# A Trainium2 kernel of two spectral and two dense layers: first layernorm from the token rows, and finer waits at three seams

## The chip, the cores and the metric

The kernel runs on one core of one Trainium2 chip. The metric is the device time of one execution in microseconds (us), taken as the median of three runs. One execution was also recorded by the profiler, and all durations below come from that record unless a sentence says otherwise. Engine names are those of the profile: PE (matrix engine), PEld (its weight loads), DVE (vector engine), ACT (scalar engine), POOL and SP. A name with a q (SPq, POOLq, ACTq) stands for instructions in that engine's queue that issue DMAs.

## What is computed

```python
x = A_x                                       # 2048 x 1024, bf16
x = x + A(layernorm(x))                       # spectral layer
x = x + B(layernorm(x))                       # dense layer
x = x + A(layernorm(x))
x = x + B(layernorm(x))
# A(x): irfft2(rfft2(x) * (w_r + 1j*w_i)), over tokens and features
# B(x): (h * tanh(softplus(h))) @ w2  with  h = x @ w1 + b1, w1 1024 x 3584
# layernorm: (x - mean) / sqrt(var + 1e-5) over the 1024 features, no gain
```

## The kernel before

Tokens stay in SBUF as `XS`, 16 tiles of 128 tokens by 1024 features. The spectral layer does not start from `XS`. It starts from `XR`, in which a partition holds a pair (a residue of the token index, a block h of 128 features), so that each token's row lies on eight partitions. In the first layer `XR` is loaded straight from `A_x` in four quarters of 32 token columns, 8 DMAs each (`prologue`, L372). In the second it is filled from `XN` rows: the dense layer before it normalises each tile of tokens (`apply`, L493), POOL stores the tile to a DRAM scratch (`xn_store`, L505), and POOL loads it back turned (`xr_load`, L514). Tile 15 alone goes from SBUF to SBUF (`xr_direct`, L518): 8 DMAs dealt to SP, ACT and POOL in turn. `xn_out` is a ring of two buffers.

**First normalisation.** The first step s1 is 16 groups j of 8 matmuls each, 128 columns wide. The mean needs no work there, and the scale 1/sqrt(var+eps) is put into the weights: `scaled` (L586) makes 8 scaled copies of the 128 x 128 table `M0` in one DVE instruction. The variances come out of `XR` itself: per quarter q, `squares` (L552) squares the quarter on ACT (the first on DVE), `sums` (L557) adds over features by two rows of 16 matmuls against a block-ones table `BO`, `roots` (L574) reduces and takes the root. `s1_first` (L606) writes this order out by hand: quarter q+1 is prepared while the four groups of quarter q run, and `s1_evac` (L602) copies each group's PSUM to `Y`, on ACT but for two. `XS` is loaded later, 1 MB in front of the layer and 1 MB behind each of its first three steps (L880 to L883), only for the residual.

**The spectral pipeline.** After s1, eight groups g pass through s2, s3, i1 and i2, software-pipelined over 11 steps (L862 on). In the first layer `filter_bins` (L902) also builds the filter of each group from rows of `w_r` and `w_i`, which POOL loads into a ring of two (`load_wr`, L894). Every engine gets its instructions in program order, and a group waits by semaphore for exactly the resources (`Res`) that its operands name.

**Turn to the tokens.** i2 leaves group g in `U`; `u_turn` (L832) stores it to a DRAM scratch and `u_back` (L847) reads it turned into rows g, g+8, ... of `UT`. For the last group the store is cut in two halves of its 16 rows (L839), both from ACT, and the read back in two halves of the 128 columns dl, on SP and ACT (L848). The whole of `UT` is one `Res`, so the first inverse matmul `i4` (L935, PE line L943) waits for all of it. The DVE adds of L957 and the next layernorm follow.

**The dense layer** is PE at work almost without a break: L1018 (first matmul, Mish on ACT) and L1036 (second matmul, DVE adds at L1041). The last four tiles of the first dense layer close with `mm2(3, t, h)`, `apply`, and the stores and loads above (L1177 to L1186).

Of the kernel before, what the change touches and what calls it, by code (L numbers as in the profile page):

```python
# [7 lines left out]
P = 128  # L8
# [116 lines left out]
def make_tables():  # L125
# [40 lines left out]
    def by_group(t):  # L166
# [5 lines left out]
                ident=np.eye(P), BO=np.kron(np.eye(16), np.ones((8, 8))))  # L172
# [7 lines left out]
class KB:  # L180
# [122 lines left out]
    def build(self):  # L303
# [3 lines left out]
        self.con = {k: v.ap().bitcast(BF) for k, v in con.items()}  # L307
        self.u_d = nc.dram_tensor("u_scratch", (8, P, 16, P), BF, kind="Internal").ap()
# [3 lines left out]
        with ExitStack() as es:  # L312
# [27 lines left out]
            self.r_ud = [Res(f"ud{i}") for i in range(8)]  # L340
            self.r_wd = [Res(f"wd{i}") for i in range(8)]
# [17 lines left out]
    def layout(self):  # L359
        K = 1024  # L360
        self.o = dict(XR=0, Z=0, X=12 * K, T=20 * K, YK=28 * K, V=40 * K, JT=48 * K, M0=49 * K, BO=49 * K + 256, RT=50 * K, XQ=32 * K,
                      ST=51 * K, WR=54 * K, YS=56 * K, UT=64 * K, MN=64 * K, Y=96 * K, XN=128 * K, U=128 * K,
                      FT=140 * K, BT=144 * K + 512, WT=self.W1_OFF)
        self.ob = dict(AT0=0, AT1=36 * K, XT1=28 * K, XT0=120 * K, W2=64 * K, JUNK=54 * K)
        assert 149 * K <= self.W1_OFF, (149 * K, self.W1_OFF)
# [6 lines left out]
    def prologue(self):  # L372
        sp = self.sp
        self.op(self.pool, lambda e: e.memset(self.EPS[:], 1e-5), writes=[self.r_eps, self.r_warm])
        small = {}

        def load_small(name, n, prog=sp):
            b = self.alloc(name, self.o[name], [n])
            self.dma(prog, b.ap, self.con[name], name.lower(), writes=[b.res])
            small[name] = b  # L380

        self.XR = self.alloc("XR", self.o["XR"], [P, P])
        self.r_xr = []
        xv = self.x[0].rearrange("(n2 n1) (h l) -> h n2 n1 l", n2=16, l=P)
        for q in range(4):
            r = Res(f"xr{q}")
            for h in range(8):
                prog = (sp, self.pool, self.act)[h % 3] if q == 0 else (sp, self.pool)[h % 2]
                self.dma(prog, self.XR.ap[h:P:8, 32 * q:32 * q + 32, :], xv[h][:, 32 * q:32 * q + 32, :], f"xr{q}{prog.name}", parts=[r])
            self.r_xr.append(r)  # L390
            if q == 0:
                load_small("BO", P, self.act)
                load_small("M0", P, self.act)
                self.warm(ACT.Sqrt)
        self.M0, self.BO = small["M0"], small["BO"]
        self.dma(sp, self.FD[:], self.con["FD"], "fd", writes=[self.r_fd])
        load_small("JT", 4 * P)
        self.JT, self.r_jt = small["JT"].ap, small["JT"].res
        self.w1_next = 0

    def load_x(self, c, after):

        xt = self.x[0].rearrange("(t p) d -> p t d", p=P)
        self.dma(self.sp, self.XS[:, 4 * c:4 * c + 4, :], xt[:, 4 * c:4 * c + 4, :], f"x{c}", reads=after,
                 writes=self.r_xs[4 * c:4 * c + 4])
# [99 lines left out]
    def xn_store(self, j, b):  # L505
        b.unread = False
        self.dma(self.pool, self.xn_d[j], b.ap, "xw" + b.res.name[2:], reads=[b.res], writes=[self.r_xnd[j]])

    def open_xr(self):
        self.XR = self.alloc("XR", self.o["XR"], [P, P])  # L510
        self.XR.res.begin()
        self.r_xr = [self.XR.res] * 4

    def xr_load(self, j):  # L514
        self.dma(self.pool, self.XR.ap[row_of(j, 0):row_of(j, 7) + 1:4, :, :], self.xn_d[j].rearrange("n (h l) -> h n l", l=P), f"xl{j % 4}",
                 reads=[self.r_xnd[j]], parts=[self.XR.res])

    def xr_direct(self, j, b):  # L518

        b.unread = False  # L520
        for h in range(8):
            prog = (self.sp, self.act, self.pool)[h % 3]
            self.dma(prog, self.XR.ap[row_of(j, h):row_of(j, h) + 1, :, :], b.ap[:, h * P:(h + 1) * P], "xd" + prog.name,
                     reads=[b.res], parts=[self.XR.res])
# [6 lines left out]
    def copy(self, prog, dst, src, reads, writes, scale=None, parts=()):  # L531
# [6 lines left out]
        return self.op(prog, fn, reads=reads, writes=writes, parts=parts)  # L538

    def open_scales(self):  # L540


        self.XQ = [self.alloc(f"XQ{i}", self.o["XQ"] + i * 8192, [32, P]) for i in range(2)]
        self.ST = self.alloc("ST", self.o["ST"], [4, 4, 32], F32)
        self.RT = self.alloc("RT", self.o["RT"], [P], F32)
        self.MN = self.alloc("MN", self.o["MN"], [P, P])
        self.r_st, self.r_rt, self.r_mn = ([Res(f"{n}{i}") for i in range(k)] for n, k in (("st", 4), ("rt", 4), ("mn", 16)))
        for b, rs in ((self.ST, self.r_st), (self.RT, self.r_rt), (self.MN, self.r_mn)):
            for r in rs:
                r.inherit(b.res)  # L550

    def squares(self, q, prog):  # L552
        x, b = self.XR.ap[:, 32 * q:32 * q + 32, :], self.XQ[q % 2]
        fn = (lambda e: e.activation(b.ap, x, ACT.Square)) if prog is self.act else (lambda e: e.tensor_tensor(b.ap, x, x, ALU.mult))  # L554
        self.op(prog, fn, reads=[self.r_xr[q]], writes=[b.res])

    def sums(self, q, sq):  # L557

        bank = 6 + q % 2
        ps = self.PS[:, bank, 256 * sq:256 * sq + 256].rearrange("p (n l) -> p n l", l=8)  # L560
        src = self.XQ[q % 2].ap if sq else self.XR.ap[:, 32 * q:32 * q + 32, :]
        fns = [lambda e, i=i: e.matmul(ps, self.BO.ap, src[:, :, 8 * i:8 * i + 8], start=(i == 0), stop=(i == 15)) for i in range(16)]  # L562
        rb = self.r_bank[bank]
        if not sq:
            rb.begin()
        w = list(rb.prev.items()) + self.BO.res.wait_r() + (self.XQ[q % 2].res if sq else self.r_xr[q]).wait_r()
        t = None
        for i, fn in enumerate(fns):
            t = self.pe.add(fn, waits=w if i == 0 else (), inc=(i == 15))
        self.mark(self.pe, t, reads=[self.BO.res] + ([self.XQ[q % 2].res] if sq else []), parts=[rb])  # L570

    def roots(self, q):

        dve = self.dve  # L574
        st, rst, rb = self.ST.ap[:, q], self.r_st[q], self.r_bank[6 + q % 2]
        s1, s2, a, b = (st[:, i, :] for i in range(4))
        rc = self.RT.ap[:, 32 * q:32 * q + 32]
        src = self.PS[:, 6 + q % 2, :].rearrange("p (c n l) -> p c n l", c=2, l=8)
        self.op(dve, lambda e: e.tensor_reduce(st[:, 0:2, :], src, axis=mybir.AxisListType.X, op=ALU.add), reads=[rb], writes=[rst])
        self.op(dve, lambda e: e.tensor_tensor(a, s1, s1, ALU.mult), writes=[rst])  # L580
        self.op(dve, lambda e: e.scalar_tensor_tensor(b, a, -1.0 / self.D, s2, ALU.mult, ALU.add), writes=[rst])
        self.op(self.act, lambda e: e.activation(a, b, ACT.Sqrt, bias=self.EPS[:, 0:1], scale=1.0 / self.D), reads=[self.r_eps],
                writes=[rst])
        self.op(dve, lambda e: e.reciprocal(rc, a), reads=[rst], writes=[self.r_rt[q]])

    def scaled(self, j):  # L586
        n = slice(8 * j, 8 * j + 8)
        self.op(self.dve, lambda e: e.tensor_tensor(self.MN.ap[:, n, :], self.M0.ap.unsqueeze(1).to_broadcast([P, 8, P]),
                                                    self.RT.ap[:, n].unsqueeze(2).to_broadcast([P, 8, P]), ALU.mult),
                reads=[self.r_rt[j // 4], self.M0.res], writes=[self.r_mn[j]])  # L590

    def s1_mm(self, li, j, i):
        M, XR = self.M, self.XR
        ps, banks = self.PS[:, 2 * i:2 * i + 2, :].rearrange("p a b -> p (a b)"), [self.r_bank[2 * i], self.r_bank[2 * i + 1]]
        fns = []
        for q in range(8):
            n = 8 * j + q
            m = M[:] if li else self.MN.ap[:, n, :]
            fns.append(lambda e, q=q, n=n, ps=ps, m=m: e.matmul(ps[:, q * P:(q + 1) * P], XR.ap[:, n, :], m, start=True, stop=True))  # L599
        self.group(fns, reads=[self.r_xr[j // 4], self.r_m if li else self.r_mn[j]], writes=banks)  # L600

    def s1_evac(self, j, i, prog):  # L602
        ps, banks = self.PS[:, 2 * i:2 * i + 2, :].rearrange("p a b -> p (a b)"), [self.r_bank[2 * i], self.r_bank[2 * i + 1]]
        self.copy(prog, self.Y.ap[:, :, 8 * j:8 * j + 8], ps.rearrange("p (q k) -> p k q", q=8), banks, [], parts=[self.Y.res])

    def s1_first(self):  # L606
        self.open_scales()
        self.Y = self.alloc("Y", self.o["Y"], [P, P])
        self.Y.res.begin()
        act, dve = self.act, self.dve  # L610
        self.sums(0, 0)
        self.squares(0, dve)
        self.sums(0, 1)
        self.roots(0)
        for j in range(16):
            q = j // 4 + 1
            if q < 4 and j % 4 == 0:
                self.squares(q, act)
                self.sums(q, 0)
# [605 lines left out]
```

## Time and profile before

| | us |
|---|---|
| median of three runs | 1064.42 |
| lowest, highest run | 1061.64, 1064.61 |
| profiled execution: its time | 1064.61 |
| profiled execution: its span | 1062.5 |
| PE, PEld busy | 966.3, 522.9 |
| DVE, ACT, POOL busy | 341.3, 326.0, 72.8 |
| mean granted PE clock | 0.968 |

The span runs from the first to the last instruction; the 2.1 us between it and the execution's time lie outside of it. Times inside the span are counted from its start. In a list of instructions in order of time, a row has its start, its length, its engine, its line and operation, out<-in, the count of merged instructions, and in brackets how long the engine was idle before it and what released it. In the chain of waits a row has start, length and what the chain spent it on.

### The profile page before, as it was taken

The numbers are of one execution on the slowest core, as the hardware profiler recorded it, in microseconds if no ns is written. First come the engines' busy times: TensorE is split into PE (matmuls) and PEld (weight loads), VectorE is DVE, ScalarE is ACT, GpSimd is POOL, SyncE is SP. The second block draws the span as 40 slices with busy tenths as digits, with TensorE's granted clock in tenths as the row PEclk, the third lists the DMA queues.
The fourth block names the chain that finished last, engine by engine and source line by source line (L and its number), as shares of the span: only waits on it lengthen the run. The fifth ranks groups of instructions, "written<-read, shape, count | busy, mean of one in ns | idle before, by whom it ended". The sixth has DMA issues, their size and how long they took to land.

```text
span 1062.5 us, 14272 instructions
## 1 busy us (share of the span) xinstructions
PE 966.3 (91%) x6071; PEld 522.9 (49%) x6160; DVE 341.3 (32%) x678; ACT 326.0 (31%) x443; POOL 72.8 (7%) x117
## 2 busy tenths in 40 slices
PE   4679678999999999999977985899999999999998
PEld 3557566444444444444436765744444444444443
DVE  3568655260443200024325775526011100000111
ACT  3678545333000233410006863533300014341000
POOL 5033000000000000000620200000000000000000
PEclk9889969999999999999998996999999999999999
DMA  9369851446111122000951786045611122200000
GB/s 218 102 228 325 229 141 34 156 157 213 45 46 46 41 80 60 1 11 20 199 101 23 205 210 179 2 151 185 199 44 35 54 67 74 65 1 11 20 20 30
DMA packets 151279, 106.99 MB, mean 101 GB/s; under 512 B 72881, under 2 KB 130353, under 8 KB 151217
## 3 DMA queue, kind: packets, MB, share of 16 engines
q1 hardware_dynamic: 137008, 75.24, 24.7%
q0 software_dynamic: 9776, 28.84, 9.7%
q10 hardware_dynamic: 4432, 2.00, 0.8%
q8 instruction: 49, 0.80, 0.3%
q14 instruction: 14, 0.11, 0.0%
HBM read 80.81 MB, written 20.71 MB: 96 GB/s over the span
## 4 chain that ended last, share of the span: by engine, by line
PE 76%; DVE 7%; DMA 6%; ACT 5%; issue 3%; POOL 2%; SPq 0%; ACTq 0%; DVEq 0%; POOLq 0%
PE PS L1018 36%; PE PS L1036 32%; POOL ARENA L249 2%; PE PS L707 2%; DMA xn_scratch<-ARENA 1%; DVE XS L957 1%; DMA ARENA<-in_A_x_dram 1%; ACT ARENA L554 1%; DMA u_scratch<-ARENA 1%; ACT ARENA L533 1%; DVE ARENA L828 1%; ACT ARENA L759 1%; PE PS L781 1%; DMA ARENA<-u_scratch 1%; DVE ARENA L993 1%
## 5 line engine op out<-in xcount | busy, mean ns | idle before, releaser
L1018 PE MATMUL PS<-ARENA 128*128 128x512 bf16 (+1 forms) x1946 | 391.0, 360 | 10.4 <-DVE ARENA L993 7.2
L1036 PE MATMUL PS<-ARENA 128*128 128x512 bf16 x1756 | 385.5, 379 | 1.9
L1022 ACT ACTIVATE ARENA<-PS,B 128x512 bf16<-128x512 f32 (+1 forms) x248 | 159.7, 645 | 439.3 <-PE PS L1018 439.3
L1018 PEld LDWEIGHTS PS<-ARENA 128*128 128x128 bf16 x1984 | 194.1, 99 | 202.0 <-DVE ARENA L993 8.8
L1036 PEld LDWEIGHTS PS<-ARENA 128*128 128x128 bf16 x1792 | 175.3, 98 | 211.5
L1041 DVE TENSOR_TENSOR XS<-PS,XS 128x512 bf16<-128x512 f32 x64 | 44.3, 692 | 536.9 <-PE PS L1036 536.9
L957 DVE TENSOR_TENSOR XS<-PS,XS 128x512 bf16<-128x512 f32 (+1 forms) x40 | 29.1, 790 | 82.5 <-PE PS L943 82.5
L461 DVE BATCH_NORM_STATS2 BN<-XS 128x6 f32<-128x512 bf16 x84 | 54.7, 677 | 1.2
L943 PE MATMUL PS<-MT,ARENA 128*128 128x32 bf16 (+1 forms) x768 | 24.6, 189 | 27.5 <-DMA ARENA<-u_scratch 24.3
L943 PEld LDWEIGHTS PS<-MT,ARENA 128*128 128x128 bf16 x768 | 23.3, 101 | 31.0 <-issue 25.4
L759 ACT ACTIVATE ARENA<-PS 128x1024 bf16<-128x1024 f32 x32 | 33.3, 1042 | 8.6 <-PE PS L755 8.6
L707 PE MATMUL PS<-FD,ARENA 128*128 128x256 bf16 (+1 forms) x256 | 33.5, 278 | 2.5 <-DVE ARENA L537 1.3
L249 POOL DMA_DIRECT2D xn_scratch<-ARENA x15 | 8.2, 550 | 391.1 <-DVE ARENA L500 391.1
L788 ACT ACTIVATE ARENA<-PS 128x1024 bf16<-128x1024 f32 x32 | 33.3, 1041 | 4.1 <-PE PS L781 4.1
L781 PE MATMUL PS<-ARENA 128*128 128x256 bf16 x256 | 33.2, 273 | 0.5 <-DMA ARENA<-c_bt 0.4
L562 PE MATMUL PS<-ARENA 128*128 128x256 bf16 x128 | 19.4, 319 | 14.7 <-DMA ARENA<-in_A_x_dram 12.0
L433 ACT ACTIVATE RS<-MV,EPS 128x1 f32<-128x1 f32 x6 | 1.7, 289 | 97.1 <-DVE MV L464 96.2
L533 ACT ACTIVATE ARENA<-PS 128x1024 bf16<-128x1024 f32 x23 | 22.4, 1027 | 25.4 <-PE PS L599 25.3
L763 DVE TENSOR_TENSOR ARENA<-ARENA 128x1024 bf16<-128x1024 bf16 x32 | 22.0, 688 | 24.2 <-ACT ARENA L759 24.1
L781 PEld LDWEIGHTS PS<-ARENA 128*128 128x128 bf16 x256 | 24.6, 98 | 10.3 <-DVE ARENA L770 1.0
L707 PEld LDWEIGHTS PS<-FD,ARENA 128*128 128x128 bf16 x256 | 24.5, 100 | 7.9 <-DVE ARENA L537 3.0
L802 PE MATMUL PS<-ARENA,BD 128*128 128x256 bf16 x192 | 25.9, 273 | 1.3 <-DVE ARENA L828 1.1
(74 smaller groups left out, 528.3 us busy)
## 6 DMA issues: line engine op xcount, KB each, us to landing
ARENA<-in_B_w_dram SPq DMA_DIRECT2D x56, 512.0 KB, 4.0
ARENA<-in_B_w_dram SPq DMA_DIRECT2D x56, 256.0 KB, 4.4
u_scratch<-ARENA SPq DMA_DIRECT2D x14, 512.0 KB, 3.5
ARENA<-u_scratch SPq DMA_DIRECT2D x14, 512.0 KB, 6.0
XS<-in_A_x_dram SPq DMA_DIRECT2D x4, 1024.0 KB, 9.7
w_scratch<-ARENA POOLq DMA_DIRECT2D x8, 512.0 KB, 7.1
ARENA<-w_scratch POOLq DMA_DIRECT2D x8, 512.0 KB, 5.7
out_dram<-XS SPq DMA_DIRECT2D x16, 256.0 KB, 2.0
```

Of the source, the lines that this page charges most:

```text
L461: self.op(self.dve, lambda e: e.bn_stats(self.BN[:, j, 6 * h:6 * h + 6], self.XS[:, j, 512 * h:512 * h + 512]), reads=[self.r_xs[j]], part ...
L533: fn = (lambda e: e.activation(dst, src, ACT.Copy)) if scale is None else \
L707: fns.append(lambda e: e.matmul(dst, at(r), FD[:, t:t + n], start=start, stop=stop))
L759: self.op(act, lambda e: e.activation(x.ap.rearrange("p a b -> p (a b)"), ps, ACT.Copy, scale=SIG), reads=banks, writes=[x.res])
L781: fns.append(lambda e, c=c, part=part: e.matmul(ps[:, c * 256:(c + 1) * 256], yk.ap[:, part, c * P:(c + 1) * P], t[:, (128, 0)[part]:(384, ...
L788: self.op(act, lambda e: e.activation(v.ap[:, :, i, :], src, ACT.Copy), reads=banks, parts=[v.res])
L943: fns.append(lambda e, l=l: e.matmul(ps[:, w * l:w * l + w], self.UT.ap[:, u0 + l, :], self.MT[:, 8 * lo:8 * lo + w], start=True, stop=True))
L957: self.op(self.dve, lambda e: e.tensor_tensor(xs, src, xs, ALU.add), reads=rb, parts=self.r_xs[lo:lo + nb])
L1018: fns.append(lambda e, db=db, bank=bank, fl=fl: e.matmul(PS[:, bank, 0:w], wb.ap[:, db, fl * P:(fl + 1) * P], x.ap[:, db, tok], start=(db ...
L1022: self.op(act, lambda e, bank=bank, ft=ft: e.activation(at.ap[:, ft, tok], PS[:, bank, 0:w], ACT.Mish, bias=self.B1[:, ft:ft + 1]), reads= ...
L1036: fns.append(lambda e, i=i, ft=ft: e.matmul(PS[:, bank, :], at.ap[:, ft, t * P:(t + 1) * P], W2[ft].ap[:, h * 512:(h + 1) * 512], start=(i ...
L1041: self.op(dve, lambda e: e.tensor_tensor(xs, PS[:, bank, :], xs, ALU.add), reads=[self.r_bank[bank]], writes=[self.r_xs[j]])
```

## The change

The diff does four things.

1. **First layernorm.** The variances are taken from `XS` instead of `XR`. `XS` is loaded first, by 4 DMAs of 1 MB on SP ahead of everything else; the `XR` quarters follow (quarter 0 all on SP, the others half on SP and half on POOL, POOL's behind the arrival of the last `XS` tile). `first_scales` takes 10 tiles' statistics on DVE and 6 on ACT, then one root for all 16 tiles, one transpose on PE and two copies, which gives `RT`. `scaled` becomes 8 small instructions per group, 5 on DVE and 3 on ACT, issued four groups ahead. The evacuations of s1 alternate between DVE and ACT. The squares, the sums, the roots per quarter, the table `BO`, and the later loads of `XS` with their gates are gone.
2. **Last group's turn.** `UT` has four `Res`, one per quarter of dl. The half 0 of the last group's rows is read back as soon as its store has landed, in two DMAs on SP; half 1 in four DMAs, a quarter of dl each, on ACT and SP in turn. `i4` waits for the quarters that it reads.
3. **Last tile's rows.** `xr_direct` sends 16 DMAs of 64 tokens in place of 8 of 128, first half of the tokens first, and the `XR` of the second layer has one `Res` per half.
4. **Late stores.** `xn_store` of tiles 12 to 14 is issued by SP instead of POOL.

```diff
 def prologue(self):
+    self.warm(ACT.Sqrt)
+    for c in range(4):
+        self.dma(sp, self.XS[:, 4*c:4*c+4, :], xt[:, 4*c:4*c+4, :], f"x{c}", writes=self.r_xs[4*c:4*c+4])
+    load_small("M0", P, BF)
+    load_small("IDF", P, F32)
...
-    prog = (sp, self.pool, self.act)[h % 3] if q == 0 else (sp, self.pool)[h % 2]
+    prog = self.pool if q and h % 2 else sp      # POOL's read self.r_xs[15] first
...
 def xn_store(self, j, b):
-    self.dma(self.pool, self.xn_d[j], b.ap, ...)
+    prog = self.sp if j >= 12 else self.pool
+    self.dma(prog, self.xn_d[j], b.ap, ...)
 def xr_direct(self, j, b):
-    for h in range(8):
-        prog = (self.sp, self.act, self.pool)[h % 3]
-        self.dma(prog, self.XR.ap[row_of(j,h):row_of(j,h)+1, :, :], b.ap[:, h*P:(h+1)*P], ..., parts=[self.XR.res])
+    for i in range(16):
+        half, h = i // 8, i % 8
+        n = slice(64*half, 64*half+64)
+        prog = (self.sp, self.act, self.pool)[i % 3]
+        self.dma(prog, self.XR.ap[row_of(j,h):row_of(j,h)+1, n, :], b.ap[n, h*P:(h+1)*P], ..., parts=[self.r_xr[2*half]])
...
+def first_scales(self):
+    for j in range(0, 16, 4):
+        n = 2 if j % 8 else 3
+        for i in range(n):
+            self.stats_dve(j + i)
+        for i in range(n, 4):
+            self.stats_act(j + i)
+        self.sums_to_mv(j + n, 4 - n)
+    self.root(0, 16)
+    rt = self.alloc("RT", self.o["RT"], [16, 8], F32)
+    self.op(dve, tensor_copy(rt, RS[:, 2, :] broadcast to 16 x 8))
+    self.group([transpose(self.PS[:, 7, 0:P], rt, self.IDF)])
+    self.op(dve, tensor_copy(rt, self.PS[:, 7, 0:P]))
...
 def scaled(self, j):
-    self.op(self.dve, tensor_tensor(MN[:, 8 columns, :], M0 broadcast, RT broadcast, mult))
+    for q in range(8):
+        n = 8 * j + q
+        if q % 3 == 1:
+            self.op(self.act, activation(MN[:, n, :], M0, Copy, scale=rc[:, n:n+1]))
+        else:
+            self.op(self.dve, tensor_scalar(MN[:, n, :], M0, rc[:, n:n+1], None, mult))
 def s1(self, li):
+    for j in range(4 if not li else 0):
+        self.scaled(j)
+    for j in range(16):
+        (8 matmuls of group j; copy to Y on ACT if j is odd, else on DVE)
+        if not li and j + 4 < 16:
+            self.scaled(j + 4)
...
 def u_turn(g, half):                              # g == 7
+    if half == 0:
+        u_back(6)
+    self.dma(act, self.u_d[g][:, h, :], u.ap[:, h, :], ..., writes=[self.r_ud7[half]])
+    if half:
+        u_last()
+def u_last():
+    back(sp, 0, 0, 2)                             # (engine, half of rows, first quarter of dl, quarters)
+    back(sp, 0, 2, 2)
+    for q in range(4):
+        back((act, sp)[q % 2], 1, q, 1)
...
-    if li == 0 and step < 3:
-        gate = Res("gate")
-        gate.set_w(self.pe, self.pe.count)
-        self.load_x(step + 1, [gate])
...
 def i4(...):
-    self.group(fns, reads=[self.UT.res, self.r_mt], writes=rb)
+    self.group(fns, reads=self.r_ut[u0 // 32:(u0 + n - 1) // 32 + 1] + [self.r_mt], writes=rb)
```

## The prediction

> **What bounds the kernel now.** I read the page's 40 slices (26.6 us each) first, to see where PE is not full.
>
> ```profile
> PE   4679678999999999999977985899999999999998
> DMA  9369851446111122000951786045611122200000
> ```
>
> PE is busy 9 tenths or more through both dense layers. The holes are slices 0 to 2 (start), 4 to 6 and 24 (turn to the tokens), 20 and 21 (return to the spectral layer). So a change outside of PE can only win there; I took each hole in order of time. First the list of instructions of 0 to 75 us:
>
> ```profile
> 28.46 3.61 ACT L554 ACTIVATE ARENA<-ARENA 128x4096 bf16<-128x4096 bf16 x1
> ...
> 32.13 1.92 PE L562 MATMUL PS<-ARENA 128*128 128x256 bf16 x16 [0.77 <-ACT ARENA L554]
> ...
> 36.07 4.56 DVE L588 TENSOR_TENSOR ARENA<-ARENA 128x1024 bf16<-128x1024 bf16 x4
> ...
> 57.34 1.89 PE L707 MATMUL PS<-FD,ARENA 128*128 128x256 bf16 x8 [1.32 <-DVE ARENA L537]
> ```
>
> Squares (3.61), their sums (1.92), then roots and four scalings (4.56) form a chain that comes round every 10.8 us, once per quarter: the squares start at 17.6, 28.5 and 39.3. `XR` itself was complete near 22 us, where POOL's wait for quarter 3 ends. The first s2 matmul comes at 57.34 because of this chain, not because of the load. Then the chain of waits:
>
> ```profile
> 61.37 7.51 DMA ARENA<-in_A_w_i_dram
> ...
> 126.58 5.18 DMA u_scratch<-ARENA
> 131.84 4.66 DMA ARENA<-u_scratch
> 136.74 1.03 PE PS L943 x32
> ```
>
> Filter rows for group 2 hold the pipeline up once. At the turn, the last half store and then the whole read back lie bare; the second layer repeats both (5.46 and 4.72). Last, the instructions around 553 us:
>
> ```profile
> 542.17 0.55 DVE L500 TENSOR_SCALAR ARENA<-XS,MV,RS 128x1024 bf16<-128x1024 bf16 x1 [1.07 <-DMA xn_scratch<-ARENA]
> 543.44 0.58 POOL L249 DMA_DIRECT2D xn_scratch<-ARENA  x1
> 548.71 1.09 POOL L249 DMA_DIRECT2D ARENA<-xn_scratch  x1 [4.69 <-DMA xn_scratch<-ARENA]
> 549.79 0.58 POOL L249 DMA_DIRECT2D xn_scratch<-ARENA  x1
> 553.80 1.85 SPq L249 DMA_DIRECT2D ARENA<-ARENA  x3
> 553.80 2.14 ACTq L249 DMA_DIRECT2D ARENA<-ARENA  x3
> 554.77 1.10 POOL L249 DMA_DIRECT2D ARENA<-xn_scratch  x1 [4.40 <-DMA xn_scratch<-ARENA]
> 555.86 1.13 POOL L249 DMA_DIRECT2D ARENA<-ARENA  x2
> 562.52 8.03 PE L599 MATMUL PS<-M,ARENA 128*128 128x128 bf16 x104 [11.62 <-DMA ARENA<-ARENA]
> ```
>
> POOL's queue alternates a store with a load that waits for it. Tile 15 is ready at 553.8, yet tile 14's load and POOL's two direct pieces go out behind it, and s1 starts at 562.52.
>
> **Part 1, the first layernorm.** Prices:
>
> ```profile
> L461 DVE BATCH_NORM_STATS2 BN<-XS 128x6 f32<-128x512 bf16 x84 | 54.7, 677 | 1.2
> L500 DVE TENSOR_SCALAR ARENA<-XS,MV,RS 128x1024 bf16<-128x1024 bf16 x48 | 25.0, 543 | 2.1 <-DMA xn_scratch<-ARENA 1.1
> ```
>
> *Arrival.* A single `XS` megabyte took 8.3 us at best, beside other loads; while three of them ran (62 to 75 us) the DMAs moved about 400 GB/s. At 350 GB/s 1.05 MB is 3.0 us; with 0.74 until SP's first issue, 0.37 for it and some 1.5 until bytes flow (in this profile near 2 us), tiles 0 to 3 are there at 5.6, the last at 14.6. The upper bound is 0.74 + 8.3 = 9.0.
> *Statistics.* In a row at 142 us one tile on DVE takes 1.45 (two half tiles and the aggregate); 10 make 14.5. The three small operations of `sums_to_mv` took 0.53, four times 2.1. From 5.6 that ends at 22.2. ACT's 6 tiles at 2.35 make 14.1 beside it. Then root (0.3), reciprocal (0.25, from 0.35 for 32 columns), copy (0.3), transpose, copy (0.3), four handovers of 0.1: 2.0 to about 24.2. The profile has no f32 transpose: between 0 and 1.9 (the 16 bf16 ones at 146 us); I take 0.4.
> *Scaling and s1.* The 128x128 scaling is not in the profile. On DVE its pace c lies between 0.13 (a statistic behind an aggregate, 143.76 to 143.89) and 0.46 (two L500 rows end to end take 1.00, of 543 ns each). A 128x8 TENSOR_SCALAR takes 172 ns; by size between that and L500 it is 0.22 long, less the 0.08 by which neighbours overlap: 0.14 to 0.19. I take 0.18, nearer to the small row. DVE then has 20c for the first four groups, 12 times 5c for the others, six copies at 1.18 between them and two at the end (2.4): 24.2 + 9.5 + 80c = 48.1. ACT has per two groups six scalings of 0.31 (0.2 fixed, 128 columns of 0.83 ns) and a copy of 0.93, 2.8, under DVE's 3.0. PE's 16 matmuls take 2.1 even at the low clock.
> *`XR`.* It moved about 235 GB/s in the first 20 us. 4.19 MB with `FD` and two small tables are 21 us behind 14.6, so quarter 3 is there at 36; group 12 asks for it near 40. It is covered, by about 4 us.
> s2 starts at 48.1, not 57.3: **9.2 less** (13.2 to -13.2 by c alone; 3.4 less of it with the late arrival).
> The old `XS` megabytes also shared the DMAs with the filter rows of group 2. Without them these should take 4 to 5.5 instead of 7.5. PE would gain up to 3.1 there, but DVE was busy until 68.88 and gains only 1.2 (its copy L923 to 71.5): I take **2.0**, bounds 0 and 3.1.
>
> **Part 2, the turn.** The last half store stays at 131.8 (ACT's queue and 99% busy DMAs). Then only 64 KB per quarter are read where 512 KB were. A read with eight rows per DMA, as the new ones have, is in the profile on POOL's queue only: a tile's turned load, 256 KB, 5.7 us, where a store of the same size takes 2.3. So some 3.4 us per 256 KB are its data, 0.85 a quarter: 2.3 + 0.85 = 3.2 against 4.7. Against that, half 0's 256 KB went out at some 130.3 and share the engines: 0.3 more. **1.2 per layer, 2.4**. Bounds per layer: 2.2 (quarter at 2.5) and -1 (half 0, at 130.3 + 5.7 = 136 and then four quarters, is what is late). Quarters 1 to 3 come each behind a DVE add of 1.16, which covers them.
> The Trainium skill, "DMA: Bandwidth & Descriptors", section on why a DMA increments its semaphore by 16, says that a DMA uses the largest number of engines up to 16 that divides the slowest dimension of both sides. By it eight rows run on 8 engines and 16 rows on all 16; cutting the rows in halves would halve the rate, which speaks against this part. At half the rate 256 KB are an estimated 2.2 us and the gain 1.4 rather than 2.2 a layer; the load's 5.7 us agrees in sign.
>
> **Parts 3 and 4, the return.** Stores 12 and 13 go from SP when `apply` ends (518.3, 530.4) instead of 536.7 and 543.4, store 14 near 541.7 (the 1.07 wait goes too); SP's queue is empty there (140.6 us of waiting for L500). POOL's loads then queue only behind each other; the last is issued near 545 and lands by 551. DVE's `apply` of tile 15 still ends at 553.78, PE's work sets it. Of the 16 direct DMAs the first eight are three on SP (0.62 each), three on ACT (0.71), two on POOL (0.57): the last goes out at 555.2. Landing took 4.3 (SP) to 5.9 (POOL) beside the load of tile 14, and 2.4 is the median of the DMA transposes of 128x128 blocks; I take 3.3. s1 at 558.7 instead of 562.5: **3.8 less**; bounds 1.9 (landing 5.4) and 4.9 (2.4). The second half, eight more issues, lands by 560.5; group 8 of s1, at 0.65 a group, asks at 562.
>
> **Sum.** 9.2 + 2.0 + 2.4 + 3.8 = 17.4 off the profiled 1064.6 gives 1047.2. That execution stands 0.2 above the median, so I say **1047**. About 0.3% is what a measurement of this kernel can tell from no change.
>
> **Rivals.**
> *A, the `XR` load becomes the bound.* It now starts 13 us later. For it: half goes through one queue, SP's, whose issues took up to 5 us each when the queue was full. Against: SP and POOL together kept 235 GB/s. At half that rate quarter 3 comes at 14.6 + 42 = 57, s2 at 60; 17.4 turns to 5.5: 1059.
> *B, the seams give nothing* since DMAs are full there (99% until 132) or eight rows are slow: 11.2 less, 1053.
> *C, slower: the 128 small scalings.* 80 of them on DVE stand in the place of 16 big ones of 1.21. If each costs a fixed price like L500 (c = 0.46), s2 starts at 70.5, 13.2 late, less 8.2 from elsewhere: 1069.6. It decides from 33.7 + 80c = 57.3 + 8.2, c = 0.40. Against: 8-column operations took 0.17.
> *D, cheaper scalings* (0.13) and clear seams: 4 plus 4 more, 1039.
> *E, the change leaves its waits in place*: if half 0's read or the second half of tile 15 comes last, each seam moves rather than goes; that ends within B.
>
> **How the numbers follow.** Forecast (1042 to 1052) 0.62, A 0.08 with milder forms of it (1053 to 1059) 0.07, B 0.08, C 0.07, D 0.08. Leaving out most of C and the ends of A and D, the range is 1037 to 1057. Only C ends slower (0.06) or close to equal, with A's worst (0.03); faster 0.91.
>
> **What would show it.** Right: first L707 near 48, DVE without gaps from 24 on, DVE scalings near 0.2 us; no stall at the third filter; `i4` about 3.2 us behind the last store's landing; s1 of layer two near 558.7. Wrong: PE or DVE waiting for a DMA into `ARENA` in s1 (A), `i4` 4.5 or more behind the store (B), scalings above 0.4 (C).

## Result and profile after

| | before | changed |
|---|---|---|
| median, us (4 runs each) | 1064.51 | 1047.49 |
| lowest, highest | 1061.64, 1067.35 | 1046.63, 1048.44 |
| profiled execution, its span | 1064.61, 1062.5 | 1046.63, 1044.8 |

The ratio is 0.984, with a 95% interval of 0.9812 to 0.9869. Where did the 17.7 us of span go? I cut both profiles at the same events: the first s2 matmul, the last store of the turned rows (ACTq), the first `i4` matmul, the first direct piece of tile 15, and the first matmul of s1 in the second layer.

| stretch, us | before | changed | difference | predicted |
|---|---|---|---|---|
| start to first s2 | 57.34 | 46.39 | -10.95 | -9.2 |
| s2 to last store, layer 1 | 69.24 | 67.02 | -2.22 | -2.0 |
| last store to `i4`, layer 1 | 10.16 | 10.46 | +0.30 | -1.2 |
| `i4` to tile 15's first piece | 417.06 | 416.72 | -0.34 | 0 |
| that piece to s1, layer 2 | 8.72 | 4.14 | -4.58 | -3.8 |
| s1 to last store, layer 2 | 72.25 | 72.14 | -0.11 | 0 |
| last store to `i4`, layer 2 | 10.39 | 10.46 | +0.07 | -1.2 |
| `i4` to the end | 417.36 | 417.48 | +0.12 | 0 |

The slices of the changed kernel's page (26.1 us each):

```profile
PE   0799489999999999999979957999999999999998
DMA  9779822464111121001941874145611112200000
```

PE now stands still through the whole first slice, is 7 tenths busy in the second and 9 or more in the next two. The list of instructions of the start shows why that pays:

```profile
6.34 1.29 DVE L460 BATCH_NORM_STATS2 BN<-XS 128x6 f32<-128x512 bf16 x2 [6.34 <-DMA XS<-in_A_x_dram]
...
22.36 0.31 ACT L432 ACTIVATE RS<-MV,EPS 128x16 f32<-128x16 f32 x1 [1.61 <-DVE MV L454]
...
24.19 3.34 DVE L579 TENSOR_SCALAR ARENA<-ARENA 128x128 bf16<-128x128 bf16 x20
...
27.44 1.22 DVE L602 CAST ARENA<-PS 128x1024 bf16<-128x1024 f32 x1
...
43.99 2.34 DVE L602 CAST ARENA<-PS 128x1024 bf16<-128x1024 f32 x2
...
46.39 1.89 PE L675 MATMUL PS<-FD,ARENA 128*128 128x256 bf16 x8 [1.19 <-DVE ARENA L602]
```

Statistics run from 6.3 to 22.3, scales are there at 24.2, and from then to 46.3 DVE works without a gap: 80 small scalings and 8 copies. The price of a scaling, from the groups by shape of the first 50 us:

```profile
L579 DVE TENSOR_SCALAR ARENA<-ARENA 128x128 bf16<-128x128 bf16 x80 | 13.6, 251 | 0.0
```

251 ns is one's length, but neighbours overlap: the first 20 start at 24.19 and the copy behind them at 27.44, so their pace is 0.163. At the turn, the chain of waits:

```profile
113.41 4.98 DMA u_scratch<-ARENA
118.41 5.22 DMA ARENA<-u_scratch
123.86 1.03 PE PS L919 x32
```

The read back takes 5.22 where it took 4.66, although the first `i4` needs a quarter of it. At the return, the list of instructions:

```profile
533.51 1.06 POOL L249 DMA_DIRECT2D ARENA<-xn_scratch  x1 [7.72 <-DMA xn_scratch<-ARENA]
...
540.59 3.79 SPq L249 DMA_DIRECT2D ARENA<-ARENA  x6
540.59 3.57 ACTq L249 DMA_DIRECT2D ARENA<-ARENA  x5
540.85 2.70 POOL L249 DMA_DIRECT2D ARENA<-ARENA  x5 [6.28 <-DVE ARENA L499]
...
544.73 8.23 PE L594 MATMUL PS<-M,ARENA 128*128 128x128 bf16 x104 [7.05 <-DMA ARENA<-ARENA]
```

POOL's last turned load leaves 7 us ahead of the direct pieces (it left 1 us behind them), and POOL waits for tile 15 as the others do.

### The profile page after: what moved, and what is told of

Its sections match the earlier page's. It is cut to its first block, busy times and chain, and to the rows that moved or that the text cites. A ratio compares the mean times of both kernels' runs of the same rounds, so it can differ in the third digit from the quotient of the medians.

```text
span 1044.8 us, 14118 instructions
## 1 busy us (share of the span) xinstructions
PE 951.7 (91%) x5944; PEld 510.5 (49%) x6033; DVE 350.9 (34%) x776; ACT 336.4 (32%) x503; POOL 71.1 (7%) x114
## 4 chain that ended last, share of the span: by engine, by line
PE 80%; DVE 9%; ACT 6%; DMA 3%; issue 1%; ACTq 0%; DVEq 0%
PE PS L994 37%; PE PS L1012 37%; DVE BN L460 2%; ACT ARENA L727 2%; PE PS L675 2%; DVE XS L933 1%; DVE ARENA L579 1%; DVE ARENA L796 1%; DMA ARENA<-u_scratch 1%; DMA u_scratch<-ARENA 1%; ACT ARENA L710 1%; DVE ARENA L969 1%; DVE ARENA L602 1%; PE PS L919 1%; ACT ARENA L798 1%
## 5 line engine op out<-in xcount | busy, mean ns | idle before, releaser
L460 DVE BATCH_NORM_STATS2 BN<-XS 128x6 f32<-128x512 bf16 x104 | 67.2, 675 | 7.6 <-DMA XS<-in_A_x_dram 6.3
L441 ACT ACTIVATE ARENA<-XS 128x1024 bf16<-128x1024 bf16 x24 | 25.3, 1055 | 37.3 <-DVE XS L933 32.4
L727 ACT ACTIVATE ARENA<-PS 128x1024 bf16<-128x1024 f32 x32 | 33.9, 1060 | 8.5 <-PE PS L723 8.5
L756 ACT ACTIVATE ARENA<-PS 128x1024 bf16<-128x1024 f32 x32 | 33.9, 1061 | 3.7 <-PE PS L749 3.7
L749 PE MATMUL PS<-ARENA 128*128 128x256 bf16 x256 | 33.2, 273 | 0.1
L499 DVE TENSOR_SCALAR ARENA<-XS,MV,RS 128x1024 bf16<-128x1024 bf16 x48 | 25.0, 543 | 1.0
```

Of the source, the lines that this page charges most:

```text
L460: self.op(self.dve, lambda e: e.bn_stats(self.BN[:, j, 6 * h:6 * h + 6], self.XS[:, j, 512 * h:512 * h + 512]), reads=[self.r_xs[j]], part ...
L727: self.op(act, lambda e: e.activation(x.ap.rearrange("p a b -> p (a b)"), ps, ACT.Copy, scale=SIG), reads=banks, writes=[x.res])
L749: fns.append(lambda e, c=c, part=part: e.matmul(ps[:, c * 256:(c + 1) * 256], yk.ap[:, part, c * P:(c + 1) * P], t[:, (128, 0)[part]:(384, ...
L756: self.op(act, lambda e: e.activation(v.ap[:, :, i, :], src, ACT.Copy), reads=banks, parts=[v.res])
```

## Experiments

All ratios are to the kernel before. Milestones are from one profile of each kernel; the same code ahead of a milestone repeats within 0.3 us for the start, but within 1.3 us for the stretch from s2 to the last store (66.7 to 67.9), so differences of that stretch under this are not read. The return of the changed kernel's code repeats between 4.1 and 4.6, its turn between 10.4 and 10.6, but for one of 9.09 (see the end). The label in brackets is the run's name, as the expectations use it.

**The seams alone** (`e9_seams_only`). The kernel before with parts 2 to 4 of the change, the first layernorm left as it was.

> The kernel before (variances from the spectral row) with the three finer seams alone. Theory from the two traces (first layer 13.2 less, turns 0.4 more, return 4.6 less): 1064.5 - 4.2 = 1060.3 us. Rival (the seams bring most of it and the first layer little): 1050 us or less.

Measured: 1061.24 us, ratio 0.9974 (0.9961 to 0.9986). By the ratio some 2.8 us (1.5 to 4.2) come from the seams, where 4.2 were expected; the rest of the 17, by subtraction, is the first layernorm's. In its profile s2 starts at 57.05, the return takes 4.14, so the whole 4.6 less, and the turns 10.46 and 10.56.

**One large scaling instead of eight small ones** (`e8_big_scale`).

```diff
-    8 per group: 5 tensor_scalar on DVE, 3 activation on ACT
+    self.op(self.dve, tensor_tensor(MN[:, n, :], M0 broadcast, rc[:, n] broadcast, mult))
```

> The changed kernel with one DVE instruction per group of s1 for the scaled weights (the 1.13 us form of the kernel before) in place of 5 small ones on DVE and 3 on ACT. Theory (DVE's work paces s1 from 24 us on): 16 times 1.13 and 8 copies make 27.5 instead of 22.1, first s2 5.2 us later, 1052.7 us. Rival (ACT paces it, which loses 14.8 us of scalings): first s2 at most 1 us later or earlier, 1047 to 1048 us.

Measured: 1053.38 us, ratio 0.9893 (0.9876 to 0.991); s2 starts at 51.43, 5.04 later. In its list of DVE's instructions a round of two groups lasts 3.40 (a copy from 42.22, the next from 45.62) where the changed kernel's lasts 2.76:

```profile
42.22 1.22 DVE L597 CAST ARENA<-PS 128x1024 bf16<-128x1024 f32 x1
43.35 2.35 DVE L573 TENSOR_TENSOR ARENA<-ARENA 128x1024 bf16<-128x1024 bf16 x2
45.62 1.22 DVE L597 CAST ARENA<-PS 128x1024 bf16<-128x1024 f32 x1
```

So DVE paces s1 once the scales are known, and sharing the scalings out is worth 5 of the 11 us at the start. The other 6 are left with the large form too: it starts s2 6 us earlier than the kernel before. They belong to the rest of part 1, the sums out of the loop and half of the copies on DVE; no run parts these two.

**The `XS` megabytes put back** (`e4_reload_xs`). Three of them are loaded again, behind the first three steps, as before. This adds work and changes no value.

> The changed kernel, and three of the four XS megabytes are loaded once more (same bytes) by SP behind the first three steps of the first layer, as the kernel before loads them. Adds work, takes none away. Theory (these megabytes shared the DMAs with the filter rows): matmul of the third filter waits 3 us again for its rows, the stretch from the first s2 to the last store is 2.2 us longer, 1049.7 us. Rival (that stretch is shorter for another reason): 1047.5 us.

Measured: 1049.2 us, ratio 0.9869 (0.9847 to 0.9891), and 68.98 from s2 to the last store. The waits of its first filters:

```profile
PE PS L894 <- DMA ARENA<-in_A_w_i_dram: 1.8, 1, 1.8
```

The wait is back, at 1.8 where 3 was expected (it was 3.1 before, and none in the changed kernel). The mechanism holds; its size is 1.1 to 2.3 us by the spread of that stretch.

**The old turn** (`e3_old_turn`). Last group read in two DMAs of 16 rows behind both stores, one wait for all.

> The changed kernel with the turn of the kernel before: the last group's read in two DMAs of 16 rows by halves of dl, behind both half stores, one wait for all. Theory (the finer turn gained nothing): i4 5.0 us behind the landing, 1046.5 to 1047.5 us. Rival (the turn gave the 1.2 us a layer of the prediction, and something else took it back): 1050 us.

Measured: 1046.62 us, ratio 0.9842 (0.9824 to 0.986). The last store to `i4` takes 10.01 and 10.04, and `i4` starts 5.0 us behind the landing, as the theory said. The changed kernel's 10.46 is 0.4 more; against the same turn in the kernel before (10.16 and 10.39) it is 0.3 and 0.1 more. So the finer turn gained nothing and cost up to 0.4 us a layer.

**16 rows, quarters of dl** (`e1_rows16`).

```diff
-    back(sp, 0, 0, 2); back(sp, 0, 2, 2)      # half 0 of the rows, ahead
-    for q in range(4): back((act, sp)[q % 2], 1, q, 1)
+    for q in range(4): back((act, sp)[q % 2], q)      # all 16 rows of quarter q, behind both stores
```

> The changed kernel, with the last group's turned read cut by quarters of dl only: four DMAs of 16 rows and 128 KB each, on ACT and SP in turn, all behind both half stores. Theory (eight rows per DMA use half of the DMA engines, and half 0's bytes stand before half 1's on the same engines): about 260 GB/s instead of 105 while the read runs, the first i4 about 3 us behind the last store's landing instead of 5.4, 4.6 us less over the two layers, 1043 us. Rival (a fixed latency of the read sets the wait, so its form doesn't matter): i4 5.2 to 5.5 us behind the landing, 1047.5 us.

Measured: 1045.51 us, ratio 0.9827 (0.9809 to 0.9845); the stretch takes 8.96 and 8.86, `i4` 4.0 and 3.9 us behind the landing. That is most of the gain, not all. Part of what is missing is order again: by the semaphore updates in the trace SP's quarter 1 landed first (122.14), ACT's quarter 0, for which `i4` waits, behind it (122.78). The stretches in which the last group is read, of the changed kernel and of this one (the last two columns are the DMA share, which can pass 1 since packets overlap, and GB/s):

```profile
119.50:122.50 3.00, 0.00 (x0) 0.00 (x0) 0.00 (x0) 0.00 (x0) 0.00 (x0) 0.50 0.73 115
```

```profile
120.50:122.30 1.80, 0.00 (x0) 0.00 (x0) 0.00 (x0) 0.00 (x0) 0.00 (x0) 0.50 1.29 237
```

Eight rows per DMA move at half the rate of sixteen, with little more than half of the DMA share. The Trainium skill's page "DMA: Bandwidth & Descriptors" says in its section "Why a DMA increments its semaphore by 16 and not by 1" that a DMA runs on the largest number of engines up to 16 that divides the slowest dimension of both sides, so eight rows use 8 and sixteen use 16. The trace agrees: while its data lands, an eight-row read updates its semaphore 8 times, a sixteen-row read 16 times. But the rate alone doesn't say which of the two costs the wait: the rate, or half 0's bytes in front.

**Eight rows, but nothing in front** (`e2_rows8_late`). Every quarter by two DMAs of eight rows, on ACT and SP at once, behind both stores.

> As e1_rows16, but every quarter is read by two DMAs of eight rows, one on ACT and one on SP, all behind both half stores: the same bytes and waits as e1_rows16, only the rows per DMA differ. Theory: 105 to 130 GB/s and about 0.6 of the DMA engines busy again, the first i4 some 4 us behind the landing (128 KB at 105 GB/s are 1.2 us and not 0.5), the last quarter later still, 1045 to 1047 us. Rival (half 0 in front is all that hurts, not the eight rows): as e1_rows16, 1043 us.

Measured: 1045.18 us, ratio 0.9828 (0.9811 to 0.9846); 8.77 and 8.81. The read is as slow as in the changed kernel:

```profile
119.50:122.50 3.00, 0.37 (x14) 0.40 (x15) 0.00 (x0) 0.00 (x0) 0.00 (x0) 0.50 0.61 126
```

and yet `i4` starts 1.7 us earlier. With the same eight rows at the same rate, the order alone is worth 1.7 us. The semaphore updates of the two traces show it. In the changed kernel half 0's two reads landed at 122.03 and 123.28, and only then the first quarter of half 1, at 123.62; `i4` followed at 123.86. Here the first quarter was complete at 121.78, and `i4` followed at 122.13. In front of that quarter the changed kernel sends 256 KB of half 0, for all of dl; at 115 GB/s that is 2.3 us. The theory's own figures came out (126 GB/s, 3.8 us behind the landing, 1045.2 us), and so did what the rival said of the comparison, the same time as `e1_rows16`; but that run had the wrong quarter in front, so the two differ in order as well as in rows.

**The same bytes as 16 rows of 16 columns** (`e10_rows16_narrow`). Eight DMAs of 64 KB in the same order; only the shape differs from the last.

> The changed kernel, last group read back by eight DMAs of 16 rows and 16 columns dl, on SP and ACT in turn, behind both half stores. Same bytes per DMA (64 KB), same order of quarters and same waits as e2_rows8_late; only the shape differs, 16 rows of 16 columns for 8 rows of 32. Theory (eight rows halve the rate, and the first i4 waits for the bytes that stand before it): the first 128 KB take 0.5 us instead of 1.2, the first i4 comes 3.1 us behind the last store's landing, 0.7 us earlier than e2_rows8_late in each layer, and the last one 2 us earlier; 1043.5 to 1044.5 us. Rival (the rows per DMA do not matter, only that nothing stands before the first quarter): as e2_rows8_late, i4 3.8 us behind the landing, 1045.2 us.

Measured: 1044.45 us, ratio 0.9816 (0.9795 to 0.9836); 8.37 and 8.57, the read at 187 GB/s. `i4` starts 3.5 and 3.6 us behind the landing, between the theory's 3.1 and the rival's 3.8: the rows give 0.2 to 0.4 us a layer of the 0.7 expected. From the last store to the first matmul of the dense layer the old turn takes 21.9 and 22.0, the changed kernel 22.4 and 22.3, this one 20.3 and 20.5. Its median is the lowest of all runs here. Its interval overlaps those of the changed kernel and of the two runs above; the 2 us a layer against the changed kernel are shown by the profiles.

**Stores back on POOL** (`e5_pool_stores`). Parts 1 to 3 only.

> The changed kernel with the stores of tiles 12 to 14 back in POOL's queue, the direct rows of tile 15 still in halves. Theory (most of the 4.6 us at the return comes from POOL's queue, which had a load and two direct pieces behind tile 15): POOL's last turned load goes out behind tile 15 again, s1 of the second layer starts 3 to 4.5 us later than in the changed kernel, 1050.5 to 1052 us. Rival (the halves bring it): 1047.5 to 1048.5 us.

Measured: 1050.87 us, ratio 0.9872 (0.9853 to 0.989). From tile 15's first piece (541.49) to s1 7.37 us. POOL's instructions:

```profile
542.03 1.08 POOL L249 DMA_DIRECT2D ARENA<-xn_scratch  x1 [4.64 <-DMA xn_scratch<-ARENA]
543.11 2.69 POOL L249 DMA_DIRECT2D ARENA<-ARENA  x5
```

The last load is behind tile 15 again, and beside it the half pieces take longer to land (DMA issues of 541 to 545):

```profile
ARENA<-ARENA SPq DMA_DIRECT2D x5, 16.0 KB, 4.3
ARENA<-ARENA ACTq DMA_DIRECT2D x5, 16.0 KB, 4.5
ARENA<-ARENA POOLq DMA_DIRECT2D x4, 16.0 KB, 3.9
```

**Whole rows of tile 15** (`e6_whole_rows`). Stores on SP, eight pieces of 128 tokens, one wait.

> The changed kernel with tile 15's rows in eight whole DMAs and one wait for all of them, the stores of tiles 12 to 14 still on SP. Theory (SP's stores bring most): s1 starts where it did or up to 1 us later, 1047.5 to 1048.5 us. Rival (the halves bring it): 3 us later, 1050.5 us.

Measured: 1050.82 us, ratio 0.9873 (0.9855 to 0.989); 7.17 us. So this theory fell and its rival held: either edit alone leaves 3 of the 4.6 us undone, and only both bring them. POOL's queue was free here; the pieces themselves were late:

```profile
ARENA<-c_ft POOLq DMA_DIRECT2D x1, 192.0 KB, 5.1
ARENA<-ARENA SPq DMA_DIRECT2D x3, 32.0 KB, 4.4
ARENA<-ARENA ACTq DMA_DIRECT2D x3, 32.0 KB, 5.3
ARENA<-ARENA POOLq DMA_DIRECT2D x2, 32.0 KB, 4.1
```

In the changed kernel the half pieces land in 2.1 to 2.5 (DMA issues of 540 to 545):

```profile
ARENA<-ARENA SPq DMA_DIRECT2D x6, 16.0 KB, 2.4
ARENA<-ARENA ACTq DMA_DIRECT2D x5, 16.0 KB, 2.5
ARENA<-ARENA POOLq DMA_DIRECT2D x5, 16.0 KB, 2.1
```

**Whole rows with POOL's next table load held back** (`e11_whole_late_table`), to see whether the table in the first line above is what delays them.

> e6_whole_rows (tile 15 in eight whole DMAs) with POOL's load of the forward table of group 2 in the second layer held until the matmuls of s1 are done. Theory (that table load, issued by POOL just behind the direct pieces, takes the DMA engines before the last pieces have moved): s1 starts 4.5 to 5.5 us after the first direct piece is issued instead of 7.2, 1048.5 to 1049.5 us. Rival (whole rows are slow by themselves): 7.2 us again, 1050.8 us.

Measured: 1050.62 us, ratio 0.9871 (0.985 to 0.9893); 6.33 us, the pieces landing in 4.4 to 4.6. Neither number came: by the profile the table takes 0.8 of the 3 us, the rest stays with the whole pieces; the two times cannot be told apart. The landings tell what the halves do: the last of all pieces came 5.9 us after the first issue here and 6.5 in the changed kernel, whose table load was not held. All 256 KB are no faster in halves; the halves let s1 start on the first.

**Narrow turn and held table together** (`e12_narrow_late_table`).

> e10_rows16_narrow with the table load of e11_whole_late_table held in the same way, tile 15 still in halves. Theory: the first half lands before the table load anyway, so s1 starts 4.1 us after the first direct piece as before; only the second half can come earlier, 0 to 0.5 us less than e10_rows16_narrow. Rival (the table, coming later, is missed by the pipeline): up to 5 us more.

Measured: 1045.01 us, ratio 0.9814 (0.9792 to 0.9836); 4.60 to s1, as without (4.62). The last piece landed 5.5 us after the first issue in place of 6.5, but s1 had not waited for it. The table is neither missed nor in the way once the rows are halved.

## Why the prediction was right, and where it was not

- **Right as a whole, by its largest term, and to the half microsecond by luck.** 1047 was predicted, 1047.49 measured. The sum was 17.4, the span lost 17.7, but the parts missed by 2.8 one way and 2.5 the other.
- **The first layernorm, right in its mechanism, 1.75 us short.** Arrival 6.3 (5.6 expected), statistics done 22.3 (22.2), scales 24.2 (24.2), pace of a scaling 0.163 (0.18), first s2 46.39 (48.1). The pace, over 80 scalings, explains 1.4 of it; the eight copies came every 1.14 instead of 1.18, which is the other 0.3. Choosing c near the small rows and not near L500 was the decision that carried the forecast. The large form's 5.0 us show that DVE is the bound, as the sum assumed.
- **`XR` hidden, right.** POOL's wait for quarter 3 ended at 34.7 (36 expected), before s1 asked for it. Rival A had no place.
- **Filter rows, right in the mechanism.** 2.22 against 2.0 in these two profiles, and the wait comes back when the megabytes do, though smaller. By the spread of the stretch (66.7 to 67.9 without the megabytes, 68.9 to 69.2 with them) the gain is 1.0 to 2.6.
- **The turn, wrong in sign.** The step that failed is "share the engines: 0.3 more". Half 0's bytes don't share, they go first, and cost 1.7 us (8.77 against 10.46). The rate of eight rows, which I had weighed as the danger, matters by 0.2 to 0.4 us. The lower bound of -1 and rival E had named this mechanism; I gave it too little weight. Rival B was right about this seam's gain, though not by its reasons, and wrong about the other.
- **The return, right in size, with one reason missing.** 4.58 against 3.8: a half piece landed in 2.4 where I took 3.3. I put the gain down to SP's stores and took the direct pieces' old 4.3 to 5.9 us as the company of tile 14's load. That company does cost: half pieces beside that load took 3.9 to 4.5 in place of 2.1 to 2.5. But the whole pieces are slow without it as well (4.4 to 4.6 with the load gone and the table held), so the halves are as necessary as the stores. Why a whole piece takes twice a half piece's time stays open.
- **Rival C**, 80 small scalings at L500's price, was excluded by 0.163 against the 0.40 from which it decides.

The turns gave 2.8 us less than the sum had for them, start and return 2.5 more; the total is closer than its parts, and nothing in the forecast made these errors cancel.

## What to carry to other kernels

A finer cut of the read helped here only where the bytes of the first consumer stood first: send what the next instruction waits for, then the rest, however early the rest is ready. Where several waits end within a microsecond or two of each other, undoing one edit can take back far more than its share (here 3.0 and 3.2 of 4.6 us for two edits), so undo each by itself before giving the gain to either. For a new small instruction, take the fixed length of the smallest rows of its kind plus its columns, less the overlap that back-to-back rows show.

## What the runs showed of the hardware

Turned reads of 256-byte pieces ran at 115 to 126 GB/s with eight rows per DMA and 187 to 256 with sixteen (187 in DMAs of 64 KB, 237 and 256 in larger ones). Eight SBUF rows filled from SBUF by 256-byte pieces took 5.9 us in 8 DMAs and 5.5 in 16 for 256 KB, from the first issue to the last landing, with the table load held; beside it 6.8 and 6.5. With neither tile 14's load nor the table beside it, the first piece of each queue landed 3.3 to 4.6 us after its issue when it had 32 KB, 2.1 to 2.5 when it had 16 KB. In the run with the megabytes put back, the second layer's turn, unchanged code, took 9.09 instead of 10.46: there, by the semaphore updates, the first quarter of half 1 landed at 627.38, ahead of half 0's second read at 628.35, where in the changed kernel it landed behind both (627.20 after 625.48 and 626.78). So the order showed as the cause once more, in code that no edit had touched.
